# RoPE attention and relu-squared MLP on one Trainium2 core: first MLP unit in halves, word joins in one two-source step, host layouts per tile

## The chip, the cores and the metric

The kernel runs on one core of one Trainium2 chip, as one program. Its time is the device time of one execution in microseconds. Shown of the kernel before are the median of three timed runs and one profiled execution.

## The reference

The inputs are q, k and v of shape 4 batches x 8 heads x 576 positions x 64, and MLP weights of 512 x 2048 and 2048 x 512 in float64. Cut to what matters:

```python
q_rot, k_rot = rotate(q), rotate(k)                  # rotary embedding on the halves of each head
scores = 1/sqrt(64) * q_rot @ k_rot.T                # 576 x 576 per head
attn = exp(scores - max); attn /= sum(attn) + 1e-9
x = (attn @ v) with heads merged                     # 2304 tokens x 512
h = x @ w_in
g = s * relu(h)**2 + b
out = g @ w_out                                      # float32
```

## The kernel before

**Tiles.** The heads are taken in 16 pairs (4 batches x 4 pairs). Each pair has nine score tiles of 128 query rows and 576 keys: tiles 0 to 3 make the first 256 tokens of the batch for both heads, tiles 4 to 7 the next 256, and tile 8 the last 64 positions of both heads. The MLP works on nine units of 256 tokens: unit 0 is tiles 0 to 3 of the four pairs of batch 0, unit 1 is tiles 4 to 7 of batch 0, and so on; unit 8 gathers the tails.

**A score tile.** TensorE makes the scores (`s_tile`), VectorE scales them and takes the extreme of each row (`s_max`, L1508), ScalarE exponentiates and sums (`s_exp`). The sum is scaled (`p_s`) and inverted on VectorE (`p_r`, L1527), one tile at a time. For most tiles the normalized weights are split into two f16 parts (`p_a`, and `p_b` on VectorE), transposed by DMA (`p_t`) and multiplied with v (`pv_sum`). The 16 tiles of unit 0 instead stay in f32: `p_norm` scales them, TensorE transposes them (`p_T`), `p_ev` copies them out of PSUM (L1597 on VectorE), and `pv32` multiplies with v once four tiles are there.

**Weights.** Each of the 32 weight tiles (16 of w_in, 16 of w_out) arrives as 64-bit words in one of two staging slots (`w64`). GpSimd writes a signed zero from the high word (`w_sign`, L1230, reading `w` into `wio`), ScalarE or GpSimd rescales the high word (`w_rebias`), and VectorE joins low and high word in two two-source steps (`w_f32`, L1290 and L1292, shown as L1233). A small matmul and a maximum give the scale (`w_gram`, `w_max`). Unit 0 reads these f32 tiles. For the other units each tile is split into two f16 parts (`w_hi`, `w_lo`); the parts of tile f are written over f32 tile f - 1, so they wait until unit 0 has read it.

**MLP units.** Unit 0 multiplies in f32 (`mlp_in`, L1693, 256 token columns, and `mlp_out`, L1730, 512 columns). Units 1 to 8 use three f16 products each (L1696 and L1733). ScalarE applies relu and square (`mlp_r`). VectorE adds the bias at the end (`out_sum`) and SP stores.

**Order.** `plan` lists all pieces with their dependencies and engines. `schedule` lays them out in time with a table of costs and due times, and the pieces are issued in that order, fixed when the program is built; each engine then executes its own list in order. All DMAs go through SP's queue. q, k and v are loaded for two pairs at a time by twelve DMAs: four for the main rows of q and k, four for their tails, and four for v.

Of the kernel before, what the change touches and what calls it, by code (L numbers as in the profile page):

```python
# [7 lines left out]
F32 = mybir.dt.float32  # L8
# [3 lines left out]
U32 = mybir.dt.uint32  # L12
AF = mybir.ActivationFunctionType
# [3 lines left out]
REBIAS = 2.0 ** -112  # L17
P_SCALE = 2.0 ** 14

PE, DVE, ACT, POOL, DMA = "PE", "DVE", "ACT", "POOL", "DMA"  # L20
ENGINES = (PE, DVE, ACT, POOL, DMA)
B, H, S, D, DM, DFF, P = 4, 8, 576, 64, 512, 2048, 128
HP, NPAIR, NF, NC = H // 2, B * H // 2, DFF // P, DM // P
MAIN, TAIL, NU, UN = 512, S - 512, 2 * B + 1, 256
PER = 9 * HP


PRM = {'z0': 2.57,
 'z1': 0.02,
 'd': 2.73,  # L30
 'ld': -1.02,
 's_lead': 89.69,
 'pab': -0.7,
 'pvlag': 2.49,
 'W0': 0.32,
 'W1': 27.83,
 'Wd': 0.48,
 'wld': 82.13,
 'sq': -5.45,
 'WP': -0.3,  # L40
 'WPd': -3.63,
 'm0': -41.22,
 'x_lead': 16.15,
 'r_lead': 128.11,
 'outlag': 8.16,
 'bias': 50.89,
 'look': 0.033024334249243475,
 'tab': -114.31,
 'fq': (0,),
 'nF': 16,  # L50
 'vz': -5.26,
 'du': [0.77, -4.74, -10.3, -1.02, -4.22, 39.84, 2.52, 17.52, 32.17],
 'ud': 21.49,
 'eng': {('g_hi', 4, 6): 'ACT',
         ('rotate', 8, 'q'): 'POOL',
         ('rotate', 15, 'q'): 'POOL',
         ('rotate', 14, 'q'): 'DVE',
         ('rotate', 4, 'q'): 'POOL',
         ('rotate', 0, 'k'): 'DVE',
         ('rotate', 11, 'k'): 'DVE',  # L60
         ('rotate', 2, 'k'): 'DVE',
         ('rotate', 7, 'q'): 'DVE',
         ('g_lo', 2, 8): 'POOL',
         ('g_lo', 4, 0): 'POOL',
         ('g_lo', 7, 4): 'POOL',
         ('g_lo', 3, 12): 'DVE',
         ('g_lo', 4, 2): 'DVE',
         ('g_lo', 6, 0): 'DVE',
         ('g_lo', 3, 10): 'POOL',
         ('g_lo', 6, 14): 'DVE',  # L70
         ('g_lo', 8, 12): 'POOL',
         ('g_lo', 2, 0): 'DVE',
         ('g_hi', 0, 4): 'ACT',
         ('rotate', 2, 'q'): 'DVE',
         ('g_hi', 1, 2): 'DVE',
         ('g_hi', 1, 10): 'ACT',
         ('g_hi', 2, 12): 'ACT',
         ('g_hi', 0, 10): 'ACT',
         ('g_hi', 7, 0): 'ACT',
         ('g_hi', 4, 14): 'ACT',  # L80
         ('g_hi', 3, 14): 'ACT',
         ('g_hi', 5, 14): 'DVE',
         ('g_hi', 2, 4): 'DVE',
         ('g_hi', 2, 2): 'ACT',
         ('g_lo', 8, 4): 'DVE',
         ('g_lo', 7, 12): 'DVE',
         ('rotate', 14, 'k'): 'DVE',
         ('rotate', 10, 'q'): 'DVE',
         ('g_lo', 1, 6): 'DVE',
         ('g_hi', 1, 6): 'DVE',  # L90
         ('g_hi', 3, 0): 'DVE',
         ('p_ev', 2, 3): 'DVE',
         ('g_hi', 2, 8): 'ACT',
         ('g_hi', 8, 6): 'ACT',
         ('g_lo', 4, 4): 'DVE',
         ('g_lo', 4, 6): 'DVE',
         ('g_lo', 7, 0): 'POOL',
         ('p_ev', 2, 0): 'DVE',
         ('g_hi', 5, 8): 'DVE',
         ('w_rebias', 0, 9): 'ACT',  # L100
         ('g_lo', 2, 2): 'DVE',
         ('g_lo', 8, 0): 'DVE',
         ('g_lo', 7, 2): 'DVE',
         ('g_hi', 4, 2): 'DVE',
         ('g_hi', 3, 10): 'DVE',
         ('g_hi', 2, 0): 'DVE',
         ('g_hi', 6, 6): 'DVE',
         ('g_hi', 7, 6): 'DVE',
         ('g_hi', 7, 10): 'ACT',
         ('g_hi', 4, 4): 'ACT',  # L110
         ('g_hi', 4, 12): 'ACT',
         ('g_hi', 2, 10): 'DVE',
         ('g_hi', 7, 4): 'DVE',
         ('g_hi', 5, 6): 'ACT',
         ('x_hi', 2): 'DVE',
         ('g_lo', 2, 10): 'DVE',
         ('g_lo', 1, 12): 'POOL',
         ('g_lo', 1, 14): 'POOL',
         ('g_lo', 6, 12): 'DVE',
         ('qk_ev', 0, 'k'): 'ACT',  # L120
         ('g_lo', 2, 6): 'DVE',
         ('g_hi', 3, 2): 'DVE',
         ('w_rebias', 0, 10): 'POOL',
         ('g_lo', 3, 8): 'POOL',
         ('g_lo', 5, 0): 'DVE',
         ('g_lo', 4, 12): 'DVE',
         ('g_lo', 3, 6): 'DVE',
         ('g_lo', 6, 10): 'POOL',
         ('g_lo', 5, 6): 'POOL',
         ('g_lo', 8, 10): 'POOL',  # L130
         ('g_lo', 3, 0): 'DVE',
         ('rotate', 7, 'k'): 'DVE',
         ('g_hi', 6, 10): 'DVE',
         ('p_norm', 1, 3): 'DVE',
         ('p_ev', 3, 3): 'ACT',
         ('g_hi', 4, 8): 'DVE',
         ('g_hi', 1, 4): 'ACT',
         ('g_hi', 8, 10): 'DVE',
         ('x_hi', 7): 'DVE',
         ('p_ev', 2, 2): 'ACT',  # L140
         ('g_hi', 2, 6): 'DVE',
         ('g_hi', 6, 12): 'ACT',
         ('g_hi', 3, 8): 'ACT',
         ('g_hi', 1, 8): 'ACT',
         ('w_rebias', 0, 2): 'ACT',
         ('g_lo', 1, 0): 'POOL',
         ('p_norm', 2, 1): 'ACT',
         ('g_hi', 6, 2): 'ACT',
         ('x_hi', 8): 'DVE',
         ('g_lo', 8, 2): 'DVE',  # L150
         ('g_lo', 7, 8): 'DVE',
         ('g_hi', 5, 12): 'ACT',
         ('g_lo', 5, 12): 'DVE',
         ('x_hi', 6): 'DVE',
         ('g_hi', 6, 8): 'ACT',
         ('g_hi', 8, 2): 'DVE',
         ('g_hi', 7, 12): 'ACT',
         ('g_hi', 8, 14): 'DVE',
         ('g_hi', 0, 8): 'ACT',
         ('g_hi', 8, 8): 'ACT',  # L160
# [1658 lines left out]
```

## Time and profile before

| | before |
|---|---|
| timed runs | 686.46, 687.12, 684.67 us; median 686.46 |
| profiled execution, span | 682.2 us |
| its time beside the span | no own time is given; the median lies 4.3 us above the span |
| TensorE busy | 619.4 us (91%) |
| VectorE busy | 503.7 us (74%) |
| ScalarE, GpSimd busy | 409.4 us (60%), 146.0 us (21%) |
| mean granted TensorE clock | 0.951 |

The span runs from the first to the last instruction. Busy times are those of the whole span; stages differ. PE is TensorE, PEld its weight load, DVE VectorE, ACT ScalarE, POOL GpSimd, SP the queue that issues DMAs. A line number can be that of a small helper (L1230, L1233, L1236), so groups are told apart by their tiles.

### The profile page before, as it was taken

The numbers are of one execution on the slowest core, as the hardware profiler recorded it, in microseconds if no ns is written. First come the engines' busy times: TensorE is split into PE (matmuls) and PEld (weight loads), VectorE is DVE, ScalarE is ACT, GpSimd is POOL, SyncE is SP. The second block draws the span as 40 slices with busy tenths as digits, with TensorE's granted clock in tenths as the row PEclk, the third lists the DMA queues.
The fourth block names the chain that finished last, engine by engine and source line by source line (L and its number), as shares of the span: only waits on it lengthen the run. The fifth ranks groups of instructions, "written<-read, shape, count | busy, mean of one in ns | idle before, by whom it ended". The sixth has DMA issues, their size and how long they took to land.

```text
span 682.2 us, 13107 instructions
## 1 busy us (share of the span) xinstructions
PE 619.4 (91%) x4846; PEld 400.6 (59%) x4846; DVE 503.7 (74%) x1208; ACT 409.4 (60%) x854; POOL 146.0 (21%) x149
## 2 busy tenths in 40 slices
PE   1975679999997999998998999999999999999997
PEld 0632345666564755675575657665666486575763
DVE  3698858899999889998895989999949962310111
ACT  2546467785676968677566886748658663142321
POOL 1822582132210242110214111030002110002100
PEclk9995658899997999999997999999999999999999
DMA  7667855698789496879789766969664753000100
GB/s 187 173 180 183 220 146 135 156 174 189 167 163 208 96 185 115 136 157 187 135 180 190 126 127 127 215 133 164 144 119 83 134 117 61 7 25 1 32 0 32
DMA packets 228624, 90.52 MB, mean 133 GB/s; under 512 B 198352, under 2 KB 223056, under 8 KB 228560
## 3 DMA queue, kind: packets, MB, share of 16 engines
q1 hardware_dynamic: 228560, 89.69, 62.5%
q8 instruction: 38, 0.62, 0.4%
q14 instruction: 26, 0.21, 0.1%
HBM read 31.82 MB, written 4.72 MB: 54 GB/s over the span
## 4 chain that ended last, share of the span: by engine, by line
PE 56%; DVE 16%; DMA 11%; issue 6%; ACT 5%; SPq 4%; POOL 2%; DVEq 0%; ACTq 0%; POOLq 0%
PE po L1733 19%; PE px L1696 17%; PE px L1573 6%; PE s L1501 6%; DMA pt<-pab 3%; DVE s L1508 3%; DVE wio L1233 3%; DVE pab L1233 3%; DMA st_q<-in_q_dram 2%; ACT p L1236 2%; PE s L1489 2%; PE po L1730 2%; DMA st_k<-in_k_dram 1%; DMA w<-in_moe_w_in_dram 1%; DMA kS<-qkT 1%
## 5 line engine op out<-in xcount | busy, mean ns | idle before, releaser
L1733 PE MATMUL po<-wio,g 128*128 128x512 f16 x768 | 185.1, 379 | 0.4 <-DVE o L1233 0.4
L1696 PE MATMUL px<-xa,wio 128*128 128x256 f16 x1536 | 184.3, 275 | 0.8 <-ACT hr L1236 0.8
L1696 PEld LDWEIGHTS <-wio 128*128 128x128 f16 x1536 | 149.4, 99 | 34.3 <-issue 3.3
L1236 ACT ACTIVATE p<-s,nm 128x576 f32<-128x576 f32 x144 | 105.5, 734 | 47.6 <-DVE s L1508 26.5
L1508 DVE TENSOR_SCALAR_CACHE_REDUCE s<-s,es 128x576 f32<-128x576 f32 x135 | 109.2, 813 | 15.2 <-PE s L1502 14.7
L1733 PEld LDWEIGHTS <-g 128*128 128x128 f16 x768 | 70.6, 98 | 74.0 <-issue 3.9
L1233 DVE SCALAR_TENSOR_TENSOR pab<-p,sum,pab 128x576 f16<-128x576 f32 x128 | 110.0, 871 | 4.4 <-ACT pab L1236 2.0
L1236 ACT ACTIVATE hr<-px,xc 128x512 f32<-128x512 f32 x64 | 43.8, 684 | 83.9 <-PE px L1696 83.8
L1717 POOL TENSOR_TENSOR g<-hr,g 128x512 f16<-128x512 f32 x28 | 34.6, 1237 | 233.0 <-ACT g L1236 139.6
L1236 ACT ACTIVATE pab<-p,sum 128x576 f16<-128x576 f32 x78 | 59.5, 768 | 24.8 <-DVE sum L1527 11.5
L1501 PE MATMUL s<-qkT 128*128 128x512 f16 (+1 forms) x150 | 54.8, 406 | 11.9 <-ACT p L1236 11.1
L1501 PE MATMUL s<-kS,qkT 128*128 128x512 f16 (+1 forms) x150 | 54.5, 402 | 7.6 <-DMA kS<-qkT 7.6
L1573 PE MATMUL px<-pt,v 128*64 128x256 f16 (+1 forms) x880 | 54.0, 251 | 7.3 <-DMA pt<-pab 7.3
L1233 DVE SCALAR_TENSOR_TENSOR wio<-w,wio 128x512 uint32<-128x512 uint32 x64 | 48.6, 769 | 13.4 <-POOL wio L1230 13.0
L1597 DVE CAST g<-hr 128x512 f16<-128x512 f32 x31 | 14.4, 464 | 58.9 <-PE po L1733 37.8
L1501 PEld LDWEIGHTS <-qkT 128*128 128x128 f16 (+1 forms) x300 | 28.6, 104 | 43.1 <-issue 13.3
L1573 PEld LDWEIGHTS <-v 128*64 128x64 f16 x880 | 38.4, 113 | 24.9 <-issue 18.8
L1230 POOL TENSOR_SCALAR pab<-p,sum 128x576 f16<-128x576 f32 x24 | 19.2, 802 | 124.9 <-DVE sum L1527 90.5
L1236 ACT ACTIVATE hr<-hr 128x512 f32<-128x512 f32 x72 | 45.1, 627 | 1.4
L1230 POOL TENSOR_SCALAR wio<-w 128x512 f32<-128x512 f32 x32 | 25.0, 782 | 91.0 <-DMA w<-in_moe_w_out_dram 42.9
L1502 PEld LDWEIGHTS <-qkT 128*128 128x128 f16 (+1 forms) x300 | 28.0, 103 | 19.2 <-issue 14.9
L1717 DVE TENSOR_TENSOR g<-hr,g 128x512 f16<-128x512 f32 x36 | 25.9, 718 | 15.6 <-ACT g L1236 15.2
(139 smaller groups left out, 903.3 us busy)
## 6 DMA issues: line engine op xcount, KB each, us to landing
w<-in_moe_w_in_dram SPq DMA_DIRECT2D x16, 512.0 KB, 4.7
w<-in_moe_w_out_dram SPq DMA_DIRECT2D x16, 512.0 KB, 3.6
kS<-qkT SPq DMA_DIRECT2D x30, 144.0 KB, 3.2
st_k<-in_k_dram SPq DMA_DIRECT2D x16, 256.0 KB, 3.1
st_q<-in_q_dram SPq DMA_DIRECT2D x16, 256.0 KB, 3.3
st_v<-in_v_dram SPq DMA_DIRECT2D x16, 256.0 KB, 4.8
out_dram<-o SPq DMA_DIRECT2D x7, 512.0 KB, 3.2
vS<-v SPq DMA_DIRECT2D x32, 64.0 KB, 2.2
```

The lines of the kernel that those rows point to most:

```text
L1230: eng.tensor_scalar(out=out, in0=in0, scalar1=s1, scalar2=s2, op0=op0, op1=op1)
L1233: nc.vector.scalar_tensor_tensor(out=out, in0=in0, scalar=scalar, in1=in1, op0=op0, op1=op1)
L1236: nc.scalar.activation(out=out, in_=in_, func=func, **kw)
L1489: nc.tensor.matmul(ps[rows, MAIN:2 * MAIN], a, d["kF"][hh, 0:512], start=True, stop=True)
L1501: nc.tensor.matmul(ps[rows, MAIN:2 * MAIN], lhs, kk[:, 4 * h:4 * h + 4], start=(n == 0), stop=(n == 1))
L1502: nc.tensor.matmul(ps[rows, MAIN - TAIL:MAIN], lhs, kk[:, 8, 64 * h:64 * h + 64], start=(n == 0), stop=(n == 1))
L1508: nc.vector.tensor_scalar(out=T["s"], in0=T["s"], scalar1=-1.0 / 8.0 if "qF" in st[pr] else st[pr]["es"], scalar2=None, op0=ALU.mult, op1= ...
L1573: nc.tensor.matmul(o[64 * h:64 * h + 64, 0:n], v_rows(pr, h, k, z), pv_rhs(pr, i, h, k), start=((z, k) == todo[0]), stop=((z, k) == todo[-1]))
L1597: nc.vector.tensor_copy(out, in_)
L1696: nc.tensor.matmul(ph, w16[0][:, f, wz, cc], X["xa"][:, xz, c], start=(c == 0 and n == 0), stop=(c == NC - 1 and n == 2))
L1717: (nc.vector if eng == DVE else nc.gpsimd).tensor_tensor(out=g[:, 1], in0=r, in1=g[:, 0], op=ALU.subtract)
L1733: nc.tensor.matmul(po, g[:, gz, jj], w16[1][:, f, wz], start=(f == 0 and i == 0), stop=(f == NF - 1 and i == 2))
```

## The change

1. *Unit 0 in halves.* The order of batch 0's tiles becomes 0 and 2 of all four pairs, then 1 and 3, then 8 and 4 to 7. Tiles 0 and 2 give the first 128 tokens of both heads. `pv32` and `o_out` run once per half with 128 columns. `mlp_in0` multiplies 128 columns at a time, so each weight tile is loaded into TensorE twice; four f tiles share one PSUM bank and one relu. `mlp_out0` keeps its 512 columns.
2. *Word joins.* The signed zero is written to the upper 16 bits of each word only, a new one-source step (`w_low`, on any of three engines) writes the lower 16 bits, and one two-source step (`w_join`) replaces the two of `w_f32`.
3. *Host layouts.* q, k, v and the weights are laid out per tile on the host. Each load is one DMA with one contiguous run per partition: one per tensor and pair, three per pair. Weights are staged in the four slots of tag `x`, shared with the units' activations, instead of two of their own; q and k have two slots and v four, each of one pair.
4. *Fewer small steps.* `p_s` and `p_r` handle two tiles in one instruction (not in unit 0 and tile 8). The inverse scale comes from an integer step in place of a reciprocal. `rotate` has three full-sized steps in place of two full and two half ones, with z written in swapped halves and a table that holds -sin.
5. *Order as a table.* The planner's costs and `schedule` are gone; order, engine of each piece and buffer slots stand in three strings. Decoded, they give 12 `w_low` to VectorE, 6 to ScalarE, 14 to GpSimd; 30 of 32 rotations to VectorE (24 before); 15 of 16 evictions of unit 0 to ScalarE (8 before).

```diff
 def tile_order():
+    out = [(hp, i) for j in range(2) for hp in range(HP) for i in (j, j + 2)]
+    out += [(hp, i) for hp in range(HP) for i in (8, 4, 5, 6, 7)]
...
     def w_sign(which, f):
-        hi = wst[which, f][:, :, 1].bitcast(F32)
-        ts_(w32[which][:, f + 1], hi, 0.0, ALU.mult, 1.0, ALU.mult, eng=nc.gpsimd)
+        ts_(halves(w32[which][:, f + 1])[:, :, 1].bitcast(BF16), wst[which, f][:, :, 1].bitcast(F32), 0.0, ALU.mult, 1.0, ALU.mult, eng=nc.gpsimd)
+    def w_low(which, f, eng):
+        o = halves(w32[which][:, f + 1])[:, :, 0]
+        x = wst[which, f].rearrange("p m t -> p (m t)").bitcast(U16).rearrange("p (m z) -> p m z", z=4)[:, :, 1]
+        if eng == DVE:
+            ts_(o, x, 13, ALU.logical_shift_right)
...
-        stt(a, lo, 29, a, ALU.logical_shift_right, ALU.bitwise_or)
-        yield
-        stt(a, hi, 3, a, ALU.logical_shift_left, ALU.bitwise_or)
+    def w_join(which, f):
         a = w32[which][:, f + 1].bitcast(U32)
+        stt(a, wst[which, f][:, :, 1], 3, a, ALU.logical_shift_left, ALU.bitwise_or)
...
+    def load_x(pr, nm):
+        t = st[pr][nm] = new(stage, nm, [P, 10 if nm == "v" else 9, D], F32, "st_" + nm)
+        nc.sync.dma_start(out=t, in_=src_of[nm][pr])
...
-        eng.tensor_tensor(out=z, in0=x, in1=sin, op=ALU.mult)
+        eng.tensor_tensor(out=z[:, :, ::-1], in0=x, in1=sin, op=ALU.mult)
         yield
         eng.tensor_tensor(out=x, in0=x, in1=cos, op=ALU.mult)
         yield
-        eng.tensor_tensor(out=x[:, :, 0], in0=x[:, :, 0], in1=z[:, :, 1], op=ALU.subtract)
-        yield
-        eng.tensor_tensor(out=x[:, :, 1], in0=x[:, :, 1], in1=z[:, :, 0], op=ALU.add)
+        eng.tensor_tensor(out=x, in0=x, in1=z, op=ALU.add)
...
+    def mlp_in0(j, f):
+        if ("h", j, f - f % 4) not in gs:
+            gs["h", j, f - f % 4] = bank()
+        ph = gs["h", j, f - f % 4][:, f % 4 * P:(f % 4 + 1) * P]
+        for c in range(NC):
+            nc.tensor.matmul(ph, wi[:, f + 1, c * P:(c + 1) * P], xs[0]["x"][:, c, j * P:(j + 1) * P], start=(c == 0), stop=(c == NC - 1))
```

## Rows read from the trace of the kernel before

**Rows 1.** The page's first lines: span, then busy us, share and instructions.

```profile
span 682.2 us, 13107 instructions
PE 619.4 (91%) x4846; PEld 400.6 (59%) x4846; DVE 503.7 (74%) x1208; ACT 409.4 (60%) x854; POOL 146.0 (21%) x149
```

**Rows 2.** Busy time of each engine by stage.

```profile
core 0: us, PE busy (x) PEld busy (x) DVE busy (x) ACT busy (x) POOL busy (x), PEclk, DMA share, GB/s
0.00:128.40 128.40, 88.42 (x478) 50.73 (x479) 94.57 (x228) 67.72 (x141) 54.80 (x61) 0.80 0.65 170
128.40:217.00 88.60, 82.00 (x551) 52.64 (x550) 83.50 (x184) 62.69 (x128) 19.07 (x22) 0.98 0.90 184
217.00:545.00 328.00, 316.24 (x2855) 207.38 (x2854) 292.23 (x733) 234.34 (x514) 58.63 (x56) 0.99 0.75 145
545.00:683.00 138.00, 132.71 (x967) 89.81 (x964) 33.44 (x65) 44.61 (x74) 13.51 (x12) 0.99 0.15 35
```

**Rows 3.** Busy time, 70 to 80 us, same columns.

```profile
70.00:80.00 10.00, 7.74 (x38) 4.49 (x39) 8.55 (x15) 4.21 (x6) 2.93 (x5) 0.50 0.88 223
```

**Rows 4.** VectorE groups: busy us, mean ns of one, idle before.

```profile
L1233 DVE SCALAR_TENSOR_TENSOR wio<-w,wio 128x512 uint32<-128x512 uint32 x64 | 48.6, 769 | 13.4 <-POOL wio L1230 13.0 <-POOL w L1230 0.4
L1508 DVE TENSOR_SCALAR_CACHE_REDUCE s<-s,es 128x576 f32<-128x576 f32 x135 | 109.2, 813 | 15.2 <-PE s L1502 14.7
L1233 DVE SCALAR_TENSOR_TENSOR pab<-p,sum,pab 128x576 f16<-128x576 f32 x128 | 110.0, 871 | 4.4 <-ACT pab L1236 2.0 <-POOL pab L1230 2.0
L1597 DVE COPY pt<-po 128x640 f32<-128x640 f32 x8 | 6.6, 821 | 0.9 <-PE po L1609 0.9
L1424 DVE TENSOR_TENSOR z<-st_k,tab 128x576 f32<-128x576 f32 x13 | 10.0, 771 | 2.9 <-DMA st_k<-in_k_dram 2.9
L1428 DVE TENSOR_TENSOR st_k<-st_k,z 128x288 f32<-128x288 f32 x13 | 5.8, 445 | 0.0
L1228 DVE TENSOR_SCALAR pab<-p,sum 128x576 f16<-128x576 f32 x26 | 14.3, 550 | 1.3 <-DMA pt<-pab 1.3
L1527 DVE RECIPROCAL sum<-sum 128x1 f32<-128x1 f32 x144 | 20.8, 153 | 5.8 <-ACT sum L1236 5.7
L1233 DVE SCALAR_TENSOR_TENSOR nat<-st_k,sc,nat 128x576 f16<-128x576 f32 x15 | 12.2, 810 | 0.6 <-ACT nat L1236 0.6
```

**Rows 5.** Timeline of TensorE: start, us, instruction.

```profile
128.42 3.70 PE L1693 MATMUL px<-x,wio 128*128 128x256 f32 x16
...
217.21 4.12 PE L1696 MATMUL px<-xa,wio 128*128 128x256 f16 x24
...
226.03 0.38 PE L1501 MATMUL s<-qkT 128*128 128x512 f16 x1
...
226.52 1.47 PE L1696 MATMUL px<-xa,wio 128*128 128x256 f16 x12
```

**Rows 6.** TensorE, weight load and ScalarE groups, same columns as rows 4.

```profile
L1693 PE MATMUL px<-x,wio 128*128 128x256 f32 x128 | 30.1, 384 | 0.0
L1693 PEld LDWEIGHTS px<-x,wio 128*128 128x128 f32 x128 | 23.6, 190 | 4.3 <-issue 0.9 <-ACT x L1236 0.2
L1696 PEld LDWEIGHTS <-wio 128*128 128x128 f16 x1536 | 149.4, 99 | 34.3 <-issue 3.3
L1236 ACT ACTIVATE p<-s,nm 128x576 f32<-128x576 f32 x144 | 105.5, 734 | 47.6 <-DVE s L1508 26.5 <-DVE sc L1228 5.5 <-DVE sum L1230 4.6
```

**Rows 7.** Chain of waits: start, us, piece.

```profile
80.17 0.60 SPq L1385
...
568.77 1.65 PE px L1573 x28
...
666.05 11.67 PE po L1733 x54
...
677.75 0.75 DVE o L1233
```

**Rows 8.** Waits in the first 128.4 us: total us, times, longest.

```profile
POOL wio L1230 <- DMA w<-in_moe_w_in_dram: 40.3, 14, 7.9
```

More of the change, by code (lines that the diff above doesn't have):

```diff
@@ L17 @@
 REBIAS = 2.0 ** -112
+FQ = (0,)
 P_SCALE = 2.0 ** 14
-PE, DVE, ACT, POOL, DMA = "PE", "DVE", "ACT", "POOL", "DMA"
+ONE = 2 ** 23
+FLOOR = 2.0 ** -14 - 0.5
+PE, DVE, ACT, POOL, DMA = "TensorE", "VectorE", "ScalarE", "GpSimd", "DMA"
 ENGINES = (PE, DVE, ACT, POOL, DMA)
+DIGITS = "ABCDEFGHIJKLMNOPQRSTUVWXYZabcdefghijklmnopqrstuvwxyz0123456789-_"
 B, H, S, D, DM, DFF, P = 4, 8, 576, 64, 512, 2048, 128
@@ L848, in unit_of, with plan, add @@
     return NU - 1 if i == 8 else 2 * (pr // HP) + i // 4
-def plan(PRM, BUFS):
+def plan():
     work, tok = [], {}
-    tile_at = tile_order()
-    slot_of = {x: n for n, x in enumerate(tile_at)}
-    last = {u: max(n for n, x in enumerate(tile_at) if unit_of(*x) == u) for u in range(NU)}
-    pick = lambda fn, key, default: PRM["eng"].get((fn, *key), default)
-    def add(t, eng, cost, fn, *a, r=(), w=(), p=()):
-        if cost is None:
-            cost = COST[fn][eng]
-        if isinstance(cost, list):
-            for i, c in enumerate(cost):
-                add(t, eng, c, fn, *a, r=r, w=w, p=p)
+    def add(engs, fn, *a, steps=0, r=(), w=(), p=()):
+        if steps:
+            for i in range(steps):
+                add(engs, fn, *a, r=r, w=w, p=p)
                 work[-1]["step"] = i
-                if (fn, i) in LOCKED:
-                    work[-1]["port"] = 2
                 if i:
@@ L885, in add, with load_w @@
             tok[k] = {"full": [n], "part": [], "read": []}
-        work.append(dict(t=t, eng=eng, cost=cost, fn=fn, a=a, step=None, deps=deps, keys=(*r, *w, *p),
-                         port=int(eng == DVE and fn in SHARED)))
+        work.append(dict(engs=engs if isinstance(engs, tuple) else (engs,), pick=isinstance(engs, tuple), fn=fn, a=a, step=None,
+                         deps=deps, keys=(*r, *w, *p)))
+    def load_w(which, f):
+        add(DMA, "load_w", which, f, w=[("x", "w", which, f), ("hi", which, f)])
@@ L1034, in plan @@
-    M0 = slot_of[HP - 1, 3] + PRM["m0"]
-    add(PRM["tab"], DMA, (.97, 1.0, 1.1, 2), "load_tab", w=[("tab",)])
-    for i in range(2):
-        add(PRM["sbt"], DMA, (.5, 1.0, 1.1, 1), "load_sb", i, p=[("sb",)])
-    for pr in range(HP):
-        prep(pr)
-    for f in range(NF):
-        convert(0, f)
-        convert(1, f)
-    first = {}
-    done = 0
-    for u in list(range(NU - 2)) + [NU - 1, NU - 2]:
-        first[u] = max(last[u] + 3, M0 + done) + PRM["du"][u]
-        done = max(done + PRM["ud"], first[u] - M0 + PRM["ud"])
@@ new lines, in unit @@
+            add(DVE, "out_sum", u, j, r=[("pj", u, j), ("bcs",), ("xc", u)], p=[("o", u, j), ("ot", u), ("po", u)])
+        for js in ((0,), (1,)) if u == NU - 2 else ((0, 1),):
+            add(DMA, "store", u, js, r=[("o", u, j) for j in js] + [("ot", u)])
+    add(DMA, "load_tab", w=[("tab",)])
+    for i in range(2):
+        add(DMA, "load_sb", i, p=[("sb",)])
+    for which in range(2):
+        for f in range(NF):
+            load_w(which, f)
+            convert(which, f)
+    for pr in range(NPAIR):
+        prep(pr)
@@ L1168, in tile_rope_attention__then__relu2_mlp @@
+    for c in tile_order():
+        attend(*c)
+    unit0()
+    for which in range(2):
+        for f in range(NF):
+            halve(which, f)
+    bias()
+    for u in range(1, NU):
+        unit(u)
+    return work
 @with_exitstack
@@ L1507, in s_max, with is_g, s_exp @@
         T["nm"] = small("nm%d" % T["slot"], 1, 1)
-        nc.vector.tensor_scalar(out=T["s"], in0=T["s"], scalar1=-1.0 / 8.0 if "qF" in st[pr] else st[pr]["es"], scalar2=None, op0=ALU.mult,
+        nc.vector.tensor_scalar(out=T["s"], in0=T["s"], scalar1=-1.0 / 8.0 if pr in FQ else st[pr]["es"], scalar2=None, op0=ALU.mult,
                                 op1=ALU.min, accum_out=T["nm"])
-    def s_exp(pr, i, at):
+    sums = {}
+    def is_g(pr, i):
+        return pr < HP and i < 4
+    def s_exp(pr, i):
         T = tiles[pr, i]
-        T["sum"] = small("sum%d" % slots["p"] if at == "SB" else "psum%d" % T["slot"], 1, 1)
-        T["p"] = new(pp, "p", [P, 576], F32) if at == "SB" else T["s"]
+        if is_g(pr, i) or i == 8:
+            T["sum"] = T["r"] = small("sum", 1, 4)
+        else:
+            if (pr, i // 2) not in sums:
+                sums[pr, i // 2] = small("sum2", 2, 6)
+            T["both"] = sums[pr, i // 2]
+            T["sum"] = T["r"] = T["both"][:, i % 2:i % 2 + 1]
+        T["p"] = new(pp, "p", [P, 576], F32)
         act(T["p"], T["s"], AF.Exp, bias=T["nm"], scale=-1.0, accum_out=T["sum"])
@@ L1648, in x_norm @@
         X = xs[u]
[L1649 removed]
+        X["xq"] = new(gp, "g", [P, 2, 2 * UN], F16).rearrange("p z n -> p (z n)").bitcast(BF16).rearrange("p (c n) -> p c n", c=NC)
         act(X["xq"], X["x"], AF.Square)
@@ L1762, in tile_rope_attention__then__relu2_mlp @@
     pieces = locals()
-    work, bufs = plan(PRM, BUFS)
-    steps = {}
+    work = plan()
+    order = [64 * DIGITS.index(ORDER[i]) + DIGITS.index(ORDER[i + 1]) for i in range(0, len(ORDER), 2)]
+    engs, where, at, steps = iter(PICKS), iter(SLOTS), {}, {}
+    pick = {}
+    for x in work:
+        if x["pick"] and not x["step"]:
+            pick[x["fn"], x["a"]] = {e[0]: e for e in ENGINES}[next(engs)]
     with tc.manual_schedule():
-        for n, opened in schedule(work, bufs, PRM["look"]):
+        for n in order:
             x = work[n]
             slots.clear()
-            slots.update(opened)
+            for k in dict.fromkeys(x["keys"]):
+                if k[0] in BUFS and k not in at:
+                    at[k] = slots[k[0]] = int(next(where))
             fn, a = pieces[x["fn"]], x["a"]
+            if x["pick"]:
+                a = (*a, pick[x["fn"], a])
             if x["step"] is None:
```

1401 lines of the change are left out of this document (264 added, 1137 removed).

## The prediction

> **What bounds the kernel now.** I read the page's first lines, then the busy time by stage, the groups of VectorE and TensorE, the waits, and the chain of waits. The span is 682.2 us, TensorE busy 91% of it, VectorE 74% [rows 1]. That mean hides four stages, cut at two matmuls: unit 0's first one at 128.4 and unit 1's first one at 217.2 [rows 5].
>
> Up to 128.4 us VectorE is busy 94.6 us (74%), TensorE 88.4, ScalarE 67.7 [rows 2]. TensorE works slowly here: its granted clock is 0.80 over the stage and 0.50, the 1.2 GHz level, at 70 to 80 us, after stretches in which it sat idle [rows 2, 3]. The engine that paces is VectorE, itself held up by the weight loads: GpSimd, which opens each weight tile, waits 40.3 us for them here [rows 8]. From 128.4 to 217 VectorE is busy 83.5 of 88.6 us (94%), TensorE 82.0: both full [rows 2]. From 217 to 545 VectorE has 292.2 of 328 us (89%) and TensorE 316.2; the 11.8 us that TensorE lacks are waits for attention. From 545 on TensorE alone counts. The last matmul ends at 677.7, and 4.5 us follow [rows 7].
>
> So three things can shorten the run: an earlier first matmul of unit 0, a shorter second stage, and less TensorE idle time after it. TensorE's columns do not change: halves of 128 tokens stream as many in all.
>
> The sum is made against the span; the median, 686.46 us, lies 4.3 us above it, taken as what surrounds the span in either kernel.
>
> **Stage one.** I counted, in the old order and in the new table, what VectorE executes ahead of unit 0's first matmul, and price it from [rows 4]:
> - Word steps 41 to 21: 20 x 0.769 = 15.4 us gone. A join is one two-source step instead of two. Against that, 9 of the new low-bits steps fall on VectorE. None exists before. It is a one-source operation on 512 elements; 0.55 is the nearest row (one source, 576 elements), 0.87 the dearest of the size, nothing the floor. I take 0.55: 5.0 us added.
> - Half a unit needs only tiles 0 and 2 of each pair, so fewer tiles stand ahead: 9 fewer maxima (0.813) = 7.3, and 5 fewer subtractions for pab (0.871) = 4.4 gone.
> - Evictions of transposed tiles 8 to 1, moved to ScalarE: 7 x 0.821 = 5.7 gone.
> - Rotations: 25 steps before, a quarter of each of four kinds (0.77, 0.77, 0.445, 0.445: mean 0.61) = 15.2; 31 after, all full-sized, as GpSimd hands five rotations over: 31 x 0.77 = 23.9. Added 8.7. The reversed write of z has no row; bounds 0.445 and 0.87, taken as 0.77.
> - One-column steps (sums, reciprocals, scales), 34 fewer at 0.15 = 5.1; four large ones at 0.8 = 3.2 gone.
> Sum: 41.1 removed, 13.7 added, 27.4 less. VectorE then has 94.6 - 27.4 = 67.2 us to do. At the pace of the old stage (94.6 of 128.4) unit 0's first matmul comes at **91 us**. ScalarE's list is no longer than before, GpSimd's is lighter (no rotation among it). Bounds: from 10 us on at the third stage's 89%: 84; below that nothing speaks.
>
> Loads: one DMA per tensor and pair instead of twelve per two pairs, so 48 issues against 96 on SP's queue. An issue takes 0.60 us there and stands on the chain [rows 7]. Since SP waits in order for buffers, I give this no term of its own: it is part of holding the pace, and if it is worth more, the 84 is nearer. Weights come in 4 KB rows; their staging has four shared slots instead of two.
>
> **Stage two.** Now it holds more: 31 tiles instead of 17. VectorE, new against old: 15 more maxima 12.2, 9 more subtractions 7.8, 3 casts 1.7, rotations 17 x 0.77 against 14 x 0.61 = 4.6, 7 steps of q, k and v at 0.8 = 5.6, 3 low-bits steps 1.7, one-column steps 1.5; 12 fewer word steps -9.2, 3 fewer g steps -1.8. Net +24.1, so 107.6 us. At the old 94% that is 114 us: unit 1's first matmul at **205**.
> TensorE must fit beside it. Its 82.0 grow by 14 score tiles (0.49 each, start to start [rows 5]) = 6.9, two pv sums (1.65 [rows 7]) = 3.3, and four transposed tiles and three half pv's, some 8: 100. Halving unit 0 doubles its weight loads: an fp32 matmul shows as two records, so 256 records of 128 columns stand where 128 of 256 columns were. Busy time of the old matmuls is 30.1 us, a load record 190 ns [rows 6]. If loads hide, the cost is 0; if each load paces a record, 256 x 0.19 = 48.6, +18.5. I take +7, nearer to hiding, since 128 records of 256 columns at 190 ns would be 24.3 us and disappear today. So 107 of 114: it fits, barely. ScalarE adds 13 exponentials (0.734 [rows 6]) and casts, some 35 us, to 62.7: 98 of 114.
>
> The Trainium skill, "TensorE: Matmul & The Clock Gate", section "Weight-path perf modes", grants the fast weight load only to inputs that are not FP32; its section on LDWEIGHTS gives about columns/1.2 ns, 107 ns for 128 columns. By that rule, as an estimate, loads of two passes cannot hide behind 128 columns, and the +18.5 would stand; the 190 ns record, against 99 for f16, agrees with it [rows 6], but no row shows such short fp32 matmuls back to back at the full clock. This speaks against the halves and is the second rival.
>
> **After.** From unit 1's first matmul to the last one took 677.7 - 217.2 = 460.5 us. In the new order five more score tiles (2.5) and one more pv sum (1.65) are done by then: 4.1 less. VectorE's whole run falls by about 40 us (32 joins 24.6, 56 pair reciprocals and 45 fewer sums on VectorE 15, evictions 5.7, smaller ones 16; added 12 low-bits 6.6, rotations 8, casts 6), of which some 37 fall here: in the stretch to 545 it had 89% and comes to about 80. Of TensorE's 11.8 idle us I take 8 away; bounds 0 and 11.8. What is late next is TensorE's own f16 MLP, unchanged. 460.5 - 4.1 - 8 = 448.
> Sum: 91 + 114 + 448 + 4.5 = 657.5 of span, + 4.3 = **662 us**.
>
> **Rivals.**
> 1. *Everything keeps full.* Stage one at 84, stage two at VectorE's 107.6, all idle time gone (444.6): 84 + 108 + 444.6 + 8.8 = 645. For it: more slots, fewer issues, VectorE at 94% for 88 us already once. Against: three engines at over 90% together is not seen before 217.
> 2. *The early start is given back.* fp32 loads pace the half unit (TensorE 118.5 at 94% = 126, +12), or the f16 halves of the weights, which can only be written once unit 0 has read the tile, start no earlier, so unit 1 starts at 217 as now: 674. For: the 190 ns; against: at 256 columns the same loads cost nothing that shows.
> 3. *Slower: the staging slots.* 22 weight tiles pass two slots in 128.4 us, 11.7 us a turn. The new slots are shared with the units' x: unit 0 takes one at the first half pv, so three turn. A turn now holds one more instruction and one more hand-over between in-order queues (sign, low bits, rebias, join). At 11.7 us it needs 22/3 x 11.7 = 86, inside the 91. If the turn grows to 17.5 us the first matmul stays at 128.4 and the fuller stage two comes on top: 662 + 37 = 699. It decides from 15.5 us a turn (first matmul at 115.5). Against: the extra work is under 1 us; for: VectorE's fixed order can make a turn wait for anything.
>
> **How the numbers follow.** Forecast 0.47 (its own range 652 to 672). Rival 1: 0.17. Rival 2: 0.20. Rival 3: 0.10 fully, and 0.06 in part, landing near no change. A measurement of this kernel can tell some 0.5%, 3.4 us. Faster: 0.47 + 0.17 + 0.19 = 0.83; same 0.07; slower 0.10. The range 643 to 684 leaves out the low tail of rival 1 and rival 3.
>
> **What would show it.** Right: unit 0's first matmul near 91, unit 1's first near 205, VectorE's busy sum near 464 us, TensorE full from 205 on, the same 4.5 us tail. The loads show in the fp32 matmuls of unit 0: starts 107 to 135 ns apart mean hidden, 190 mean rival 2. Rival 3 would show as VectorE's joins waiting for GpSimd and SP waiting for a staging slot. Wrong would be the forecast if the first matmul of unit 0 comes after 110, or if it comes early and unit 1 does not.

## The result, and the profile after

The changed kernel takes 647.39 us (median; 645.03 to 649.97) where the kernel before took 686.47 beside it: ratio 0.946, 95% interval 0.940 to 0.952. The profiled execution took 648.1 us, 1.8 beyond its span.

The page's first lines and the busy time by stage, cut at the two matmuls that cut the old run (columns as in [rows 1, 2]):

```profile
span 646.3 us, 13244 instructions
PE 592.6 (92%) x5054; PEld 397.6 (62%) x5054; DVE 491.7 (76%) x1043; ACT 414.5 (64%) x864; POOL 141.5 (22%) x138
```
```profile
0.00:83.90 83.90, 47.69 (x390) 31.58 (x390) 69.28 (x150) 59.36 (x126) 35.75 (x41) 0.86 0.80 245
83.90:196.40 112.50, 106.86 (x897) 73.06 (x896) 104.44 (x234) 94.68 (x199) 23.25 (x25) 0.98 0.81 183
196.40:524.00 327.60, 321.70 (x2940) 216.22 (x2939) 285.32 (x603) 222.52 (x478) 68.65 (x60) 1.00 0.66 139
524.00:647.00 123.00, 116.36 (x835) 76.75 (x832) 32.67 (x60) 37.96 (x64) 13.81 (x12) 0.99 0.15 33
```

The first matmuls of unit 0 (L819) and of unit 1 (L793), as one view of each line: count, duration in ns (least, median, most), first and last start in us.

```profile
L819 PE MATMUL px<-x,wio x256: 273/275/579, 83.9 to 171.6; 128*128 128x128 f32 x128
...
L793 PE MATMUL px<-xa,wio x1536: 269/273/283, 196.4 to 628.9; 128*128 128x256 f16 x192
```

Against [rows 2, 5]: stage one ends at 83.9 instead of 128.4 (44.5 us less), stage two lasts 112.5 instead of 217.2 - 128.4 = 88.8 (23.7 more), and from unit 1's first matmul to the last one it is 444.8 instead of 460.5 (15.7 less). The end, as a chain of waits (start, us, piece), answers to [rows 7]: the last matmul ends at 641.22, and 5.1 us follow instead of 4.5.

```profile
638.95 0.76 DVE o L359
...
639.75 1.47 PE po L863 x6
...
641.24 0.75 DVE o L359
```

So -44.5 + 23.7 - 15.7 + 0.6 = -35.9, the whole change of the span. The loss of stage two is smaller than the gain of stage one because work was moved, not only removed.

VectorE's groups that answer to [rows 4] (the join, the maximum, the subtraction for pab, the new low-bits step, the paired reciprocal):

```profile
L359 DVE SCALAR_TENSOR_TENSOR wio<-x,wio 128x512 uint32<-128x512 uint32 x32 | 25.1, 792 | 11.4 <-POOL wio L356 10.7 <-ACT wio L362 0.5 <-ACT x L362 0.2
L595 DVE TENSOR_SCALAR_CACHE_REDUCE s<-s,es 128x576 f32<-128x576 f32 x135 | 109.5, 818 | 16.9 <-PE s L589 14.8 <-ACT sum L362 1.5
L359 DVE SCALAR_TENSOR_TENSOR pab<-p,sum,pab 128x576 f16<-128x576 f32 x128 | 110.0, 878 | 7.1 <-ACT pab L362 5.2 <-POOL pab L356 1.6
...
L626 DVE RECIPROCAL sum<-sum 128x2 f32<-128x2 f32 x56 | 8.8, 158 | 6.7 <-ACT sum L362 6.3
L354 DVE TENSOR_SCALAR wio<-x 128x512 uint16<-128x512 uint16 x12 | 8.5, 712 | 1.3 <-DMA x<-in_moe_w_in_dram 1.3
```

The fp32 loads of unit 0 on TensorE's timeline: 40 matmul records start to next instruction in 163.23 - 158.66 = 4.57 us, 114 ns apart.

```profile
158.66 4.73 PE L819 MATMUL px<-x,wio 128*128 128x128 f32 x40
163.23 0.38 PE L588 MATMUL s<-qkT 128*128 128x512 f16 x1
```

Before, the 16 records of 256 columns that start at 128.42 [rows 5] gave way to the next instruction after 131.95 - 128.42 = 3.53 us, 221 ns apart:

```profile
131.95 0.38 PE L1501 MATMUL s<-qkT 128*128 128x512 f16 x1
```

So 128 columns cost 114 ns where half of 256 cost 110. The weight loads of the same 40 records, and the two groups of unit 0 after the change that answer to [rows 6]:

```profile
158.66 4.54 PEld L819 LDWEIGHTS px<-x,wio 128*128 128x128 f32 x40 [0.20 <-issue]
163.12 0.10 PEld L588 LDWEIGHTS <-qkT 128*128 128x128 f16 x1
```
```profile
L819 PE MATMUL px<-x,wio 128*128 128x128 f32 x256 | 33.7, 285 | 0.8 <-DVE wmx L427 0.6 <-ACT xt L362 0.2
L819 PEld LDWEIGHTS px<-x,wio 128*128 128x128 f32 x256 | 30.8, 196 | 4.0 <-DVE wmx L427 1.2 <-issue 1.0 <-ACT x L362 0.6
```

GpSimd's waits for w_in in stage one, total us, times and longest, fell from 40.3 [rows 8] to

```profile
POOL wio L356 <- DMA x<-in_moe_w_in_dram: 24.4, 6, 12.7
```

### The profile page after: what moved, and what is told of

It is laid out like the page before. It is cut to its first block, busy times and chain, and to the rows that moved or that the text cites. A ratio compares the mean times of both kernels' runs of the same rounds, so it can differ in the third digit from the quotient of the medians.

```text
span 646.3 us, 13244 instructions
## 1 busy us (share of the span) xinstructions
PE 592.6 (92%) x5054; PEld 397.6 (62%) x5054; DVE 491.7 (76%) x1043; ACT 414.5 (64%) x864; POOL 141.5 (22%) x138
## 4 chain that ended last, share of the span: by engine, by line
PE 56%; DVE 17%; DMA 12%; ACT 7%; issue 5%; POOL 2%; SPq 1%; DVEq 0%; POOLq 0%; ACTq 0%
PE po L863 20%; PE px L793 19%; PE px L672 6%; PE s L588 5%; DVE pab L359 4%; DMA pt<-pab 4%; DVE s L595 4%; ACT p L362 2%; DMA qkT<-nat 2%; PE po L843 2%; DVE wio L359 2%; DMA x<-in_moe_w_in_dram 2%; POOL wio L356 1%; DMA st_k<-in_k_dram 1%; DMA x<-in_moe_w_out_dram 1%
## 5 line engine op out<-in xcount | busy, mean ns | idle before, releaser
L793 PE MATMUL px<-xa,wio 128*128 128x256 f16 x1536 | 182.4, 273 | 1.3 <-ACT x L362 1.3
L793 PEld LDWEIGHTS <-wio 128*128 128x128 f16 x1536 | 148.2, 98 | 34.9 <-issue 3.5
L362 ACT ACTIVATE p<-s,nm 128x576 f32<-128x576 f32 x144 | 106.0, 736 | 67.2 <-DVE pab L359 29.6
L811 POOL TENSOR_TENSOR g<-hr,g 128x512 f16<-128x512 f32 x32 | 38.6, 1207 | 207.6 <-ACT g L362 135.0
L362 ACT ACTIVATE pab<-p,sum 128x576 f16<-128x576 f32 x69 | 52.0, 768 | 13.1 <-DVE sum L626 7.6
L356 POOL TENSOR_SCALAR wio<-x 128x512 bf16<-128x512 f32 (+1 forms) x46 | 43.6, 954 | 64.4 <-DMA x<-in_moe_w_in_dram 24.4
L588 PE MATMUL s<-qkT 128*128 128x512 f16 (+1 forms) x150 | 52.6, 388 | 5.2 <-ACT p L362 4.9
L588 PE MATMUL s<-kS,qkT 128*128 128x512 f16 (+1 forms) x150 | 52.6, 386 | 1.8 <-DMA kS<-qkT 1.8
L672 PE MATMUL px<-pt,v 128*64 128x256 f16 (+1 forms) x880 | 51.7, 247 | 1.8 <-DMA pt<-pab 1.4
L362 ACT ACTIVATE hr<-hr 128x512 f32<-128x512 f32 x68 | 42.6, 628 | 1.1
L819 PE MATMUL px<-x,wio 128*128 128x128 f32 x256 | 33.7, 285 | 0.8 <-DVE wmx L427 0.6
L811 DVE TENSOR_TENSOR g<-hr,g 128x512 f16<-128x512 f32 x32 | 22.8, 712 | 14.6 <-ACT g L362 14.3
```

The lines of the kernel that those rows point to most:

```text
L356: eng.tensor_scalar(out=out, in0=in0, scalar1=s1, scalar2=s2, op0=op0, op1=op1)
L362: nc.scalar.activation(out=out, in_=in_, func=func, **kw)
L588: nc.tensor.matmul(ps[rows, MAIN:2 * MAIN], lhs, kk[:, 4 * h:4 * h + 4], start=(n == 0), stop=(n == 1))
L672: nc.tensor.matmul(o[64 * h:64 * h + 64, 0:n], v_rows(pr, h, k, z), pv_rhs(pr, i, h, k), start=((z, k) == todo[0]), stop=((z, k) == todo[-1]))
L793: nc.tensor.matmul(ph, w16[0][:, f, wz, cc], X["xa"][:, xz, c], start=(c == 0 and n == 0), stop=(c == NC - 1 and n == 2))
L811: (nc.vector if eng == DVE else nc.gpsimd).tensor_tensor(out=g[:, 1], in0=r, in1=g[:, 0], op=ALU.subtract)
```

## The experiments

The theory of the prediction: VectorE's work sets stage one, at the pace that its feeding allows; loads, layouts and slots only hold that pace. The rival: slots and queue set stage one themselves. All runs start from the changed kernel unless said, and "first matmul" is unit 0's.

**Joins as before the change.**

```diff
-        ts_(halves(w32[which][:, f + 1])[:, :, 1].bitcast(BF16), wst[which, f][:, :, 1].bitcast(F32), 0.0, ALU.mult, 1.0, ALU.mult, eng=nc.gpsimd)
+        ts_(w32[which][:, f + 1], wst[which, f][:, :, 1].bitcast(F32), 0.0, ALU.mult, 1.0, ALU.mult, eng=nc.gpsimd)
...
     def w_low(which, f, eng):
+        return
...
+        stt(a, wst[which, f][:, :, 0], 29, a, ALU.logical_shift_right, ALU.bitwise_or)
         stt(a, wst[which, f][:, :, 1], 3, a, ALU.logical_shift_left, ALU.bitwise_or)
```

> The word conversion as before the change: VectorE joins a word in two two-source steps, and no low-bits steps run. Ahead of unit 0's first matmul that gives VectorE 21 more joins and takes 9 low-bits steps off it: 21 x 0.77 - 9 x 0.71 = +9.8 us; later 11 x 0.77 - 3 x 0.71 = +6.3. If VectorE's work sets the first two stages (my theory): first matmul of unit 0 at 94 to 97 instead of 83.9, unit 1's first at 208 to 216 instead of 196.4, total 657 to 666. If the weight loads or the staging slots set the pace and VectorE only waits on them (rival): both matmuls within 3 us of the changed kernel's, total under 651.

656.6 us, ratio 0.958 (0.952 to 0.964). The lines of the two first matmuls, and stage one:

```profile
L821 PE MATMUL px<-x,wio x256: 272/275/582, 88.9 to 181.6; 128*128 128x128 f32 x128
...
L795 PE MATMUL px<-xa,wio x1536: 269/273/283, 206.2 to 637.7; 128*128 128x256 f16 x192
```
```profile
0.00:88.90 88.90, 49.74 (x391) 32.65 (x391) 80.13 (x161) 58.58 (x123) 25.02 (x32) 0.83 0.75 231
```

Between the two: VectorE took 10.8 us more work into stage one and lost 5.0 there; the other half went into its idle time (90% busy instead of 83%). By unit 1 it had lost 9.8, and it kept nearly all of that to the end (span +8.8).

**q, k and v in their original layout**, ten DMAs a pair (the kernel before had twelve for two pairs, so this goes further back than it).

```diff
-        nc.sync.dma_start(out=t, in_=src_of[nm][pr])
+        main, tail = src_of[nm][bb, 2 * hp:2 * hp + 2, 0:MAIN, :], src_of[nm][bb, 2 * hp:2 * hp + 2, MAIN:S, :]
+        if nm == "v":
...
+        else:
+            nc.sync.dma_start(out=t[:, 0:8].rearrange("p (h t) d -> p h (t d)", h=2), in_=main.rearrange("h (p t) d -> p h (t d)", t=4))
+            for z in range(2):
+                nc.sync.dma_start(out=t[64 * z:64 * z + 64, 8], in_=tail[z])
```

> q, k and v are read from their original layout, ten DMAs for a pair instead of three (160 issues on SP's queue instead of 48), in pieces of 256 bytes to 1 KB; all else as in the changed kernel. If the layout only lightens a queue that had time (my theory): first matmul of unit 0 within 4 us of 83.9, total 647 to 653. If the issues on SP's queue were what held the old first stage, and the single DMA per tensor is what let it shrink (rival): 28 more issues ahead of the first matmul at 0.6 us are 17 us, first matmul past 95, total 660 or more.

675.04 us, ratio 0.986 (0.981 to 0.991): the rival. The first matmul comes 13.2 us later where it priced 17; unit 1's comes 23.2 later, and the end 28.1.

```profile
L830 PE MATMUL px<-x,wio x256: 273/275/579, 97.1 to 193.0; 128*128 128x128 f32 x128
...
L804 PE MATMUL px<-xa,wio x1536: 269/273/283, 219.6 to 657.7; 128*128 128x256 f16 x192
```

VectorE has the same work ahead of the first matmul, 69.05 us against 69.28, but needs 97.1 us for it:

```profile
0.00:97.10 97.10, 53.53 (x391) 35.13 (x391) 69.05 (x152) 60.50 (x128) 32.36 (x41) 0.75 0.71 211
```

SP's queue shows what comes late. Here the second q load is issued at 13.98 us, 0.6 us apiece behind the pieces of v; in the changed kernel (second fence) it was issued at 6.98:

```profile
11.32 0.66 SPq L481 DMA_DIRECT2D st_v<-in_v_dram  x1
12.03 0.60 SPq L483 DMA_DIRECT2D st_v<-in_v_dram  x1
...
13.98 0.60 SPq L485 DMA_DIRECT2D st_q<-in_q_dram  x1
```
```profile
5.74 0.33 SPq L476 DMA_DIRECT2D st_v<-in_v_dram  x1
6.98 0.33 SPq L476 DMA_DIRECT2D st_q<-in_q_dram  x1
```

The transfers themselves are hardly slower: up to 97 us w_in's tiles land 4.9 us after their issue (median) against 4.7 in the changed kernel, and the main rows of q 3.9 against 3.9. That speaks for the issues as the cause.

**Unit 0's first matmul after both halves.** Same instructions; the order table was made anew with one more rule.

```diff
+ mlp_in0(j, f) stands behind o_out(pr, ("j", 0)) and o_out(pr, ("j", 1)) of all four pairs
```

> Same instructions, but unit 0's first matmul waits until both halves of 128 tokens are complete, as a whole unit would; the order table is re-made for it, the rest keeps its place. In the changed kernel the last piece of the second half ends at 108, so the first matmul comes at 108 to 113. In the changed kernel TensorE did only some 7 us of unit 0's work between 84 and 108. Theory A (TensorE's and VectorE's work set the end, and the half only fills TensorE's holes): those 7 us go behind, total 651 to 659. Theory B (the early start itself is the gain, all later work hangs on it): +24 us, total 668 or more. Theory C (the halves buy nothing, VectorE sets both stages): within 3 us of 647.

653.95 us, ratio 0.956 (0.950 to 0.962), whose interval overlaps the changed kernel's at its edge; spans 651.4 and 646.3.

```profile
L819 PE MATMUL px<-x,wio x256: 273/275/377, 111.3 to 177.9; 128*128 128x128 f32 x128
...
L793 PE MATMUL px<-xa,wio x1536: 269/273/283, 202.7 to 634.0; 128*128 128x256 f16 x192
```

Theory A: 27.4 us later at the first matmul, 6.3 at unit 1's, 5.1 at the end. The early start is not itself the gain; it lets TensorE do some 6 us of unit 0's work in holes of stage one and two.

**Two staging slots for the weights, then three, then two with the word steps later, then five.** In the first two the slot string changes, and with it the order table: with two slots 27 weight loads and 18 other pieces stand later in it, with three slots five loads and two word steps. So each price below is that of fewer slots in an order made for four and little changed. In short:

```diff
- weights pass slots 0, 1, 2, 3 of "x"
+ weights pass slots 0, 2 (next run: 0, 2, 3)
```

> The weights' staging is held to two of the four shared slots (0 and 2), as before the change; units keep all four. Word steps, halves and layouts as in the changed kernel. Theory (VectorE sets stage one, a turn of a slot can shrink): the turn has to be 84/10.5 = 8 us where it was 11.7 before, first matmul of unit 0 at 84 to 90, total 647 to 654. Rival (the turn keeps its 11.7 us because VectorE's order, not the slot, makes it): 21/2 x 11.7 = 123, first matmul past 110, total 665 or more.

> The weights' staging is held to three of the four shared slots (0, 2 and 3); all else as in the changed kernel. Two slots brought unit 0's first matmul from 83.9 to 128.0 and the time to 710. If a slot matters only while too few are left for a turn (theory: unit 0's x holds one of the four from the first half on anyway): first matmul at 84 to 90, total 647 to 655. If each slot buys its share (rival): first matmul at 98 to 112, total 668 to 685.

Two slots: 710.5 us, ratio 1.039 (1.033 to 1.046). Three: 658.64, ratio 0.962 (0.955 to 0.968). The line of the first matmul with two, and then with three:

```profile
L819 PE MATMUL px<-x,wio x256: 273/275/582, 128.0 to 234.8; 128*128 128x128 f32 x128
```
```profile
L819 PE MATMUL px<-x,wio x256: 272/275/582, 93.3 to 181.7; 128*128 128x128 f32 x128
```

For two slots the rival's numbers held; its reason, that VectorE's order makes the turn, is not shown by them. VectorE has 70.36 us of work in 128.0, 55%, and waits at its joins and low-bits steps (waits in that stage):

```profile
DVE wio L359 <- POOL wio L356: 24.0, 8, 5.9
DVE wio L354 <- DMA x<-in_moe_w_in_dram: 15.7, 4, 6.4
```

Three slots fell between the two expectations: 9.4 us at the first matmul, 11 in time.

> Two staging slots again, but the word steps, the loads and the gram matmuls stand later in the order table (their places stretched by 1.26), so that an engine meets a tile's step when the slot can have delivered it. In the run with two slots VectorE stood 24 us at joins whose tile had not come. If that fixed order made the price (theory): first matmul at 85 to 105, total 655 to 680. If the turn of a slot, some 12 us, makes it whatever the order (rival): first matmul past 115, total 690 or more.

753.03 us, ratio 1.101 (1.097 to 1.105): inside the rival's bounds, at the end far past them. The first matmul comes at 116.2 us, 11.8 earlier than with the first order for two slots, and unit 1's at 301.3. VectorE stands less at its joins now (17.3 us up to 130), but SP waits longer for the slots that the later joins free, 48.9 us in the same stretch, where it was 36.3 up to 128.0 with the first order for two slots:

```profile
SPq L390 <- DVE wio L359: 48.9, 15, 12.1
```

Moving the steps later did not take the price of two slots away. What the best order for two slots would give is not shown.

```diff
+def fifth(which, f):
+    return "xt" if (which, f) in ((0, 5), (0, 8), (0, 14), (1, 3)) else "x"
...
-        t = new(xp, "x", [P, NC, UN], F32).rearrange("p c n -> p (c n)")
+        t = new(xp, fifth(which, f), [P, NC, UN], F32).rearrange("p c n -> p (c n)")
```

> One step the other way: five staging slots for the weights. The buffer of the last unit's x stands empty until the first tail tiles are done, so four weight tiles (every fifth) pass through it, and from the fifth tile on each load stands in SP's queue where the load before it stood. Two slots cost 63 us, three 11 against four. If the price of a slot goes on falling by that factor (theory): first matmul of unit 0 at 82 to 84, total 643 to 648, about what a measurement can tell. If earlier weight loads push q, k and v back in SP's queue, as an early start of the weights did in the old kernel with four slots (rival): first matmul at 86 to 92, total 650 to 658.

650.33 us, ratio 0.951 (0.946 to 0.956), not to be told from the changed kernel; first matmul at 84.9, between the two expectations, the time at the rival's lower end. GpSimd's wait for w_in up to 84 us is now

```profile
POOL wio L360 <- DMA x<-in_moe_w_in_dram: 7.1, 4, 3.9
```

where it was 24.4, and nothing was won: in the changed kernel that wait did not set the time. The time by slots is 710, 659, 647, 650.

**Four slots in the kernel before.**

```diff
-        at = pick("w_at", (which, f), "w64")
+        at = "x" if f//2%2 and which==0 else "w64"
```

> The kernel before, with one line changed: w_in's tiles 2, 3, 6, 7, 10, 11, 14 and 15 are loaded into the two slots of the units' x, which stand empty then, so that w_in passes four slots instead of two; w_out keeps its two. Its own planner orders the work anew. If the slots made the old first stage (what the run with two slots in the changed kernel suggests): unit 0's first matmul at 105 to 118 instead of 128.4, total 664 to 677. If VectorE's work made it, as my prediction had it: first matmul within 4 us of 128.4, total 681 to 690.

701.21 us, ratio 1.025 (1.020 to 1.030): neither. Its planner let the weights go first, and q and k came behind them. The first f16 score matmul starts at 83.0 us where it started at 55.9 before, unit 0's first matmul at 145.8:

```profile
L1693 PE MATMUL px<-x,wio x128: 379/379/483, 145.8 to 217.5; 128*128 128x256 f32 x128
...
L1501 PE MATMUL s<-qkT x150: 376/379/637, 83.0 to 569.6; 128*128 128x512 f16 x120, 128*64 128x512 f16 x30
```

Four slots cost 17 us here, with the planner's costs and due times as they were. What they would be worth to the old kernel with an order of their own stays open.

**w_in in runs of 1 KB.**

```diff
+            nc.sync.dma_start(out=t.rearrange("p (c m) t -> p c (m t)", c=NC),
+                              in_=w_in[:, f * P:(f + 1) * P].bitcast(U32).rearrange("(c p) x -> p c x", p=P))
```

> w_in is read from its original layout in runs of 1 KB instead of 4 KB, still one DMA a tile; all else as in the changed kernel. In the kernel before, w_in's tiles landed 4.7 us after issue and w_out's 3.5. If the run length matters little beside three or four slots (my theory): first matmul of unit 0 at 84 to 87, total 646 to 651. If it makes each turn of a slot longer (rival): 16 loads over 3 slots, each 1.2 us later, 6 us: first matmul near 90, total 653 or more.

645.34 us, ratio 0.943 (0.938 to 0.948): nothing. w_in lands 5.0 us after issue, against 4.7 with 4 KB runs; the weights' layout, unlike that of q, k and v, saves no issue.

**Single sums and reciprocals.**

```diff
-        nc.vector.reciprocal(r, r)
+        for r in [both[:, i:i + 1] for i in range(both.shape[1])]:
+            nc.vector.reciprocal(r, r)
```

> Each score tile has its sum and its reciprocal in one-column instructions of its own again, where the changed kernel does two tiles in one; order unchanged. 56 more reciprocals and as many more sums, 0.07 us each from start to start where VectorE is full: 4 to 8 us of VectorE, nearly all after unit 1's first matmul. If TensorE alone counts there (my theory): total 646 to 651. If those steps stood in TensorE's way (rival: the 8 us of idle time I took off came from them): 653 to 658.

648.66 us, ratio 0.949 (0.942 to 0.955), my theory. VectorE has 78 more instructions than the 1043 of the changed kernel and 3.6 us more busy time, 46 ns each. That is a rough price, since runs with the same 1043 instructions have 487.0 to 495.0 us. Another count agrees: if each record is charged only with its time after the record before it on VectorE had ended, sums and reciprocals come to 14.4 us here and to 11.2 in the changed kernel, 41 ns for each of the 78.

```profile
PE 591.2 (92%) x5054; PEld 397.1 (62%) x5054; DVE 495.3 (77%) x1121; ACT 417.1 (65%) x898; POOL 138.1 (21%) x138
```

**Low-bits steps off VectorE.** In the string of engines, the 12 w_low of VectorE become ScalarE's:

```diff
- w_low: 12 V, 6 S, 14 G
+ w_low: 18 S, 14 G
```

> The 12 low-bits steps that VectorE executes go to ScalarE (0.77 us each there, 0.71 on VectorE), 9 of them ahead of unit 0's first matmul; order unchanged. Joins taken back onto VectorE cost about half their work in the first stage and all of it by unit 1. By that rate: first matmul at 80 to 82, unit 1's first 6 us earlier, total 638 to 644. If VectorE is no limit, or ScalarE, which also rebiases, becomes late (rival): first matmul at 84 to 88, total 646 to 652.

648.81 us, ratio 0.949 (0.944 to 0.953), first matmul at 86.2: the rival. VectorE's work ahead of it falls to 66.36 us and nothing is won. ScalarE, which also rebiases the weights, is busy 64.78 us of those 86.2 instead of 59.36 of 83.9, and the joins wait 2.3 us for it instead of 0.2; that this makes the whole loss is not shown.

**Joins, layout of q, k and v, and whole unit 0, undone together** (the three diffs above in one kernel, with the order table of the run for the whole unit 0; slots, weights' layout and paired steps stay).

> Three parts undone at once: two joins a word, q, k and v in their original layout with ten DMAs a pair, and unit 0's first matmul after both halves. Undone one by one they cost 5.0, 13.2 and 27.4 us at unit 0's first matmul and 9.2, 27.7 and 6.6 us of time (against 647.4). If they add up (each takes its own time on the path): first matmul at 126 to 132, total 686 to 695. If they share cover (rival: one engine's waiting hides another's work): first matmul at 112 to 120, total 672 to 682.

685.33 us over 10 runs, ratio to the kernel before 1.002 (0.999 to 1.005): in sum the whole gain is gone.

```profile
L832 PE MATMUL px<-x,wio x256: 273/275/583, 130.6 to 206.3; 128*128 128x128 f32 x128
...
L806 PE MATMUL px<-xa,wio x1536: 269/273/421, 232.9 to 668.4; 128*128 128x256 f16 x192
```

At the first matmul the three add up (129.5 expected, 130.6 measured); in time the sum of 43.5 comes out as 38, just under the expected range. This is not the kernel before again. Its layout of q, k and v goes further back, and unit 1's first matmul comes 15.7 us later than before the change (217.2). From there to its last matmul it takes 447.8 us, near the changed kernel's 444.8 and not the 460.5 of before. So most of the gain after unit 1's start has other causes than these three parts.

## Why the prediction was right, and where its reasons were not

The forecast was 662 us in a range of 643 to 684; 647.4 is faster, as forecast, and lies near its rival 1 (645).

*The sum.* Stage one 83.9 (91 predicted), stage two 112.5 (114), the rest 444.8 (448), tail 5.1 (4.5), around the span 1.8 (4.3). All terms but the tail erred to the same side, and stage one by most. The 4.3 was not what surrounds the span: every later execution of the kernel before took 1.7 to 1.9 us more than its span, so 2.5 of the 4.3 came from a profiled execution faster than the median. In rival 3 a turn of 15.5 us gives a first matmul at 113.7; the 115.5 named beside it takes 15.75.

Rival 1 had stage one at 84 and the rest at 444.6, and 83.9 and 444.8 were measured. The first agrees in its reason too: from 10 us on VectorE was to be 89% busy, and it was 90%; the prediction had called the 84 nearer in case the loads were worth more. Its middle term, 108, did not come (112.5). The 444.6 agrees by luck, since it took all of TensorE's idle time away, and 6.7 us of it are left.

*Stage one: the work was right, the pace was not.* Predicted: 67.2 us of VectorE at the old pace of 74%. Measured: 69.3 us at 83%. Dividing VectorE's busy time ahead of the first matmul by that matmul's time shows what moves the one and what the other:

| | VectorE work, us | first matmul, us | pace |
|---|---|---|---|
| before | 94.6 | 128.4 | 0.74 |
| changed | 69.3 | 83.9 | 0.83 |
| joins back | 80.1 | 88.9 | 0.90 |
| both halves first | 91.9 | 111.3 | 0.83 |
| q, k, v layout back | 69.1 | 97.1 | 0.71 |
| two slots | 70.4 | 128.0 | 0.55 |
| three back | 106.8 | 130.6 | 0.82 |

Half units change the work and leave the pace. The joins change the work, and half of it is taken from idle time, so my division by 0.74 overpriced them: 10.8 us cost 5.0, not the 14.7 that the division gives. SP's issues and the slots change the pace and leave the work. The step that failed is the one that gave the loads "no term of its own" and made them part of holding the old pace: with the issues put back the first matmul comes 13.2 us later and the end 27.7. That run has 160 issues for q, k and v against 96 before, so what the step from 96 to 48 is worth was not measured by itself. A term for the loads was missing, and the joins' term was too large; the two errors work against each other, and how nearly they cancel stays open.

*Rival 3 was a real limit, on the safe side.* With two slots the first matmul fell to 128.0 us, beside the 128.4 of before, and three still cost 11 us. The four slots were enough, the fifth won nothing. That 128.0 and 128.4 agree does not show that the slots made the old stage: 130.6 came with four slots, and four slots in the kernel before gave 145.8.

*Rival 2.* The 114 ns between matmul records are inside the 107 to 135 that were to mean hidden loads, though the load record itself is 196 ns long. The rival took a record's duration for the pace of the loads; but the same 40 loads follow each other just as closely (163.12 - 158.66 = 4.46 us, 112 ns each). TensorE's busy time in stage two is 106.9 us, 107 predicted, but that sum has 7 us for the loads: the matmuls of unit 0 went from 30.1 to 33.7, by 3.6, and the other 3.3 lie in work that was priced too low. So the 107 is right in part by luck. By the Trainium skill, "TensorE: Matmul & The Clock Gate", section "Weight-path perf modes — Fast Weight Load (FWL) and DoubleRow", an fp32 weight load gets no fast path, from which I had drawn that it would show; the page does not say so itself, and the trace does not agree with that conclusion for 128 columns.

*After unit 1's start.* The busy time of VectorE was to fall to about 464 us; it fell to 491.7, by 12 instead of 40. The 15 us that I took for paired reciprocals and fewer sums are the largest error that the trace shows: 0.15 us is a step's recorded duration, but charged only with the time after the record before it, all sums and reciprocals went from 15.7 to 11.2 us, so the 101 fewer are worth 4.5. The recorded mean of low-bits steps was 712 ns where I took 550.

What was bought with that term, 8 us of TensorE's idle time, came in part. From unit 1's first matmul to the last one it was idle 11.8 of 460.5 us before and 6.7 of 444.8 after. The rest of the 15.7 us is busy time, 448.7 before and 438.1 after: 10.7 us less where I had 4.1 for the work moved ahead. Some of that goes with the granted clock of the stretch, 0.99 before and 1.00 after: the same 1536 matmuls of units 1 to 8 that read w_in went from 184.3 to 182.4 us. Undoing the paired steps gave nothing back in time, so they are not what shortened the rest; which of the other edits did, no run here tells apart.

## What to carry to other kernels

Read a stage as work divided by pace, and ask of each edit which of the two it changes: the work of the pacing engine can be counted from the trace before, while its pace hangs on what feeds it (DMA issues on one in-order queue, staging slots) and has to be given a term of its own. A microsecond on an engine that is 83% busy need not be worth one: here 10.8 us put back on VectorE cost 5.0, and 2.9 taken off it gained none. A buffer is worth nothing once the wait for it sets nothing: the fifth slot here. Price short instructions by what they add to the engine's time, not by their recorded durations, which overlap.

## What the runs showed of the hardware that I had not expected

- Between 5 and 14 us an issue on SP's queue took 0.33 to 0.43 us for a load in one run per partition, and 0.60 to 0.66 for the pieces of v: there, pieces cost twice, by their number and by their price. The price is not fixed: over the whole run the issues of q in one run took 0.33 to 0.61 us, median 0.53.
- With 128 columns, fp32 matmul records follow each other at 114 ns while each weight load's record is 196 ns long.
- The granted clock of stage one was 0.86 in the changed kernel and 0.96 with five slots, with the first matmul at 83.9 and 84.9 us: in a stage where TensorE was busy 57 to 59%, the higher clock brought no earlier matmul.
- Of the 12 low-bits steps on VectorE in the changed kernel, six took 0.43 to 0.46 us and six 0.91 to 1.03. All six long ones ran beside a GpSimd instruction, and two of the short ones. The mean of 712 ns is that of two prices, and which one is paid was not predicted.
